# Merging two matmuls of a block product over 512 columns, and a mask fused with its row extremum, in a hand-ordered attention and MLP kernel

## The chip, the core and the metric

The kernel runs on one core of a Trainium2 chip. The core has engines with queues of their own: TensorE (PE; its weight loads are listed as PEld), VectorE (DVE), ScalarE (ACT), GpSimd (POOL) and SyncE (SP, which here issues nearly all DMAs). Matmuls write PSUM, which has eight banks of 128 partitions by 512 float32 columns; the other engines copy results out to SBUF. The metric is the device time of one execution in microseconds (us), less is better. A difference is told as a ratio of times with its interval.

## The reference

Attention over 4 sequences of 768 tokens with 8 heads of 64, each query seeing a window of fewer than 16 tokens to either side and 24 summaries of blocks of 32 keys; its output, 3072 tokens by 512, goes through an MLP.

```python
def _attn_ref(q, k, v):                       # q, k, v: (4, 8, 768, 64)
    ...
    k_sum = k.reshape(B, H, nb, block, D).max(axis=3)      # block = 32
    v_sum = v.reshape(B, H, nb, block, D).mean(axis=3)
    scores_l = scale * np.matmul(q, k.transpose(0, 1, 3, 2))
    mask_l = np.abs(pos[:, None] - pos[None, :]) < window  # window = 16
    scores_s = scale * np.einsum('bhsd,bhnd->bhsn', q, k_sum) + np.log(block)
    scores_all = np.concatenate([np.where(mask_l, scores_l, -1e9), scores_s], axis=-1)
    a = np.exp(scores_all - np.max(scores_all, axis=-1, keepdims=True))
    a = a / (np.sum(a, axis=-1, keepdims=True) + 1e-09)
    return np.matmul(a, np.concatenate([v, v_sum], axis=2))

def _moe_ref(x, w_in, w_out):                 # x: 3072 x 512, w_in: 512 x 2048
    h = x @ w_in
    sp = np.maximum(h, 0.0) + np.log1p(np.exp(-np.abs(h)))
    return (h * erf(sp)) @ w_out
```

## The kernel before

**Tiles.** The 3072 tokens are 6 chunks of 512 (`NCH`). A *quad* is one chunk by two heads, so there are 24 quads. A *period* k is one chunk by one group of 512 of the 2048 hidden columns, so there are 24 periods (`NPER`), four to a chunk. In period k the kernel computes the hidden tile of period k, the second product (`mm2`) of period k-1, and the attention of a later quad, so that PE has work of several kinds at all times.

**Float32 in two parts.** Values go through PE as a high part and a low part in a fast float32 format: w x = w_h x_h + w_h x_l + w_l x_h. So each product is three matmuls. In `mm2` (L936) and in the first product of the early periods (`mm1`, L780) they have 512 columns.

**Block products.** From period 8 (`FAST`) on, the first product is done by a scheme with seven products of 2 x 2 blocks instead of eight (`products`). For each half n (called a and b) of the group there are seven jobs P1 to P7, each over two slices c of the contraction. A job issues six matmuls of 256 columns (L821). P1, P6, P7 and P4 use bank b of their half, its left 256 columns only (`L`); P2, P5 and P3 use bank a. Bank b is `h1` for half a and `pB` for half b; `pA` and `pB` also hold the attention scores of a quad. Behind each job, small operations (`out1`, `out6`, ...) copy or add the bank's half into `hc`. The x blocks are in `xt` (the two parts of one slice lie side by side in one tile), and the sums and differences of x blocks in a place of the weights' tile (`place`, written by `tsplit`).

**Behind the products.** ScalarE makes softplus of `hc`, then erf (each behind a load of its function table, L1206); VectorE multiplies (`gsplit`: L912), casts to the high part (L257) and subtracts for the low part (L919), per half; these feed `mm2` of the next period. `hc` of a half has one buffer: the products of period k+1 can only be copied into it behind the subtraction of period k.

**Attention.** Scores of a quad are eight blocks of 64 queries for two heads, 120 columns each (96 window keys, 24 summaries), in the banks `pA` and `pB`. The first four quads get their mask on PE. From quad 4 (`MQ`) on, `softmax` adds the mask on VectorE (`add`, L589, two instructions of 480 columns), takes the maxima (`red`, L594) and scales them by -0.125 (L613); ScalarE takes the exponentials (`exps`, L604, eight instructions, each with its sum read out), VectorE normalises (L620), and from quad 12 on VectorE turns 32 x 32 blocks (L567), which are moved into place by 16 small copies on either engine.

**The order.** Nothing is issued as written. `P.add` collects every operation with a number, the engines it may run on with a planner's cost in us, and the resources that it reads and writes. The string `ORDER` then lists all numbers in the order of issue, made in advance; a `d` or `a` behind a number puts an operation that may run on two engines on VectorE or ScalarE. Each engine executes its own operations in that order, whatever becomes ready first. `FILL` maps numbers to a count of filler matmuls (L975, 256 bfloat16 columns of zeros into a spare bank) that PE issues ahead of that operation; this holds until the first `mm2` that needs the spare bank.

```python
for i, (m, l) in enumerate(((0, 0), (0, 1), (1, 0))):
    nc.tensor.matmul(shape, lhsT=w[m], rhs=y[l], start=first and c == 0 and i == 0, ...)
```

Of the kernel before, what the change touches and what calls it, by code (L numbers as in the profile page):

```python
# [26 lines left out]
T = 512  # L27
# [24 lines left out]
149 183 130 184 131 219 115 153 178 132 146 179 190 180 181 150a 177 185 151d 191 198 186 182a 133a 200 187d 134a 201 142 135 195a 188 202 145 136 203
143 205 189 192 206 152 196d 207 197 138d 137a 233 154 139 237 155d 140 234 157 175 248 238 199 211 144 156d 204a 158 208 212 159 242 160 235 220 239
213 227 243 223 241 214 209d 215 245 231 161d 224 247 162d 163 277 164 246 210 216 217 218 232 226 236 225 240 165 276 244 249 166 282 283 222 278
167a 168d 230 314 279 288 169 280 170 289 284 274 281d 285 350 171d 172a 221 286d 353 173 287 357 228d 250d 229d 252 352 305 366 351 256d 313 304 355
258 306 356 312 307 384 262a 293 174 354 308 294 251a 275 290 309 385a 253 361 295 291a 301 254 365 292 360 255 364 296 257d 297 342 320 315 259 316
343 317 264 318 310a 298 260 299 300 359 302 311a 319a 363 261 268a 263a 326 270 321 265 327 303 322 368d 269d 266 323 271 331 324a 267 272 344 358
347 332 345 380 369a 362 346 325 370 328 333 392 339 371 329a 393 334 375d 372 394 330 348d 395 335 373 387 349d 388 382 386 389 374d 390 273 451 340
455 376 381 367 449 336 377 453 337 338 450 378 417 454 341 398 391a 379 396a 452 399 418d 456 383 397 419 403 420 404 415 414 421 467 422 405 465 460
468 457 461 406 539 459 407 471 463 400 416d 464 401d 411 423 402 458 462 472a 408 409 410 425 469 426 473 424a 431 412 470 427 432 521 540 436 413  # L60
522 437 447 446 519 523 438 525 439 526 440 428 520 429d 433 448d 474 430 434d 444 475 441 435 476 442 443 524 466 479 480 477 445 535 487 485 478a
481 536 488a 482 486 490 489 541 491 483a 501 484 528 503 514 515 532 543 529 504 527 547d 531 505 548 530 506 545d 534 555 546 495 551d 533 556d 552
496 549d 497 557 550 498 553 537 492 507 508 509 516a 493 606 494a 538 610 499a 554 569 500 621 542 598 558 623 559 637 622 502 544 624 607 625 517
511d 560 626 510a 570 561 513 512 608 562d 612 599 585 627 638 685 574 601 600 575 587 518 576 740 628 577 588 563 605 571 611 602d 564 572a 589 565
590 573 566 609 805 613 578d 846 616 567d 614 618 629 615 591 592 593 619 568 620 931 579 630 586 635 631 653 594d 603 595d 597 617 596 654 580 639
581 632 647 640d 648 633 649 641 634 582 650 710 693 583d 604 692 712 584 696 713 636 711 694 714 697 642 715 643 716 655 698 695 717 656a 699 644 718
708 657 645 721 669 719 646a 702 722 687 651a 688 703 652 720 671 700 723 701 724 705 738 672 704 663 727 726 664 689d 706 742 658 673 659 743d 674
660 725 744 661 665 728 666 729 662a 814 675 667a 730 813 668 676 731 818 677 670 817 732 679 690 678 683 812 680d 739 816 682 681 707 733 815 709 735
756 758 734 684 691 745 757 736 746 750 759d 737 828 751 686 752 753 829 741 830 747 831 748 850 832 819 749a 851 772 754a 842 833 755 760 761 808 807
766 834 767 774 844 823 762 835 820 775 836 763 856 764 839 768 776 857 765a 769 840 777 864 821 858 841 825 837 773 809d 838 891 800d 945 822 810  # L70
770a 799 778 798 852 824 779 802 848 853 803 895 854 806 826 804 771 855 892 847 849 862 780 896 863a 827 845 801 893 781 843 897 867 785d 796a 791d
859 792a 874 795a 868 794a 787d 790a 860 811 866 784a 783d 788a 870 861 782a 869a 890 871a 786d 865a 894 793d 875a 789d 876 797d 948 872 877 878 873a
884 879 946 882 885d 888 880 883 929 900 881 947 930 949 932 939 936 926d 925d 886 927 928 943 887a 961 889 898 899 955d 962 956 941 901 933 950 934
938 942 963 940 902 951a 944 937 953a 952 967 964 957a 1050 969 954 968a 958 903 971 965 904 966 972 973 970d 975 974d 977 976d 979 978d 935a 905 981
906 980a 907 983 960 959 982 985 1051 984 987 986 908 989 1052 991 990d 910a 909d 995 915a 914d 924d 922a 996 916d 919a 911d 993 997 1036 998 988 1056
999 920d 913d 1000 917d 992a 923d 1054 1001 921d 912d 918d 1002 1003 1053 994 1004 1058 1005 1006 1039 1038 1034 1043 1031a 1041 1030d 1035 1055 1032
1044 1033 1007 1045 1046 1059 1047 1008 1061 1009 1048 1049 1060 1064 1149 1062 1066 1042 1065d 1068 1063 1069 1040a 1010 1037 1067a 1070 1011 1072
1134 1057 1071a 1074 1012 1073a 1155 1076 1075a 1013 1078 1077a 1080 1079 1023a 1082 1016d 1022a 1150 1081 1018a 1084 1083 1019a 1233 1086 1027a 1151
1028a 1015d 1088 1020a 1255 1029d 1021d 1092 1087d 1085 1090 1093 1026d 1094 1024d 1014d 1017d 1095 1089a 1025d 1153 1096 1097 1098 1091 1157 1099
1100 1152 1158 1101 1340 1154 1102 1137 1103 1136 1132 1142 1140 1127 1104 1143 1129a 1133 1144 1128 1131 1145 1105 1160 1106 1146 1147 1130 1148 1159  # L80
1163 1249 1161 1165 1138a 1141 1164a 1107 1162 1139a 1167 1168 1108 1135 1166a 1169 1109 1156 1171 1173 1170d 1172a 1110 1175 1174a 1177 1176a 1112d
1115a 1121d 1179 1111d 1123a 1125d 1124a 1181 1178 1250 1126a 1122d 1120d 1116a 1183 1182 1259 1118d 1185 1180 1113a 1251 1187 1184 1186d 1191 1260
1189 1192 1119d 1114d 1193 1117d 1253 1188d 1194 1195 1196 1190 1265 1197 1198 1199 1266 1252 1254 1200 1267 1201 1235 1202 1236 1231 1242 1228a 1239
# [78 lines left out]
def block_attention_mlp(ctx: ExitStack, tc: tile.TileContext, q_t, k_nat, k_win, v_tok, v_nat, v_win, w_in, w_out, out):  # L162
# [417 lines left out]
    def softmax(qd, banks=PA):  # L580
# [5 lines left out]
        def add(e):  # L586
            t = s["pr"] = prob[:, :, 0:NK]
            for a in range(2):
                e.tensor_tensor(t[:, NI * a:NI * a + NI], s["sc"][a][:, 0:NI * NK].rearrange("q (i c) -> q i c", i=NI), mk, op=ALU.add)  # L589
# [658 lines left out]
```

## Time and profile before

| | |
|---|---|
| runs (median of 3) | 613.16 us (612.96 to 619.82) |
| the profiled execution, its own time | 616.26 us |
| its span, first to last instruction | 614.5 us |
| mean granted TensorE clock | 0.997 |
| busy: PE, PEld, DVE, ACT | 99%, 83%, 77%, 75% |
| instructions: PE, DVE, ACT | 4720, 800, 911 |
| DMA | 150.22 MB, mean 244 GB/s |

Busy shares are means over stages that differ. The windows view gives, for each stretch of the span, the busy time of each engine with the number of its instructions, the granted clock, and the DMAs' share. In the timeline and in the chain of work a row begins with its start in us and its length; in brackets stands how long the engine was idle before it and what released it. The rows of a group have count, busy time and mean duration in ns.

### The profile page before, as it was taken

How to read it: one execution, taken by the hardware profiler on the slowest of the kernel's cores; microseconds unless marked ns; L12 is line 12 of the kernel's file. 1: busy time of each engine (PE TensorE's matmuls, PEld its weight loads, DVE VectorE, ACT ScalarE, POOL GpSimd, SP SyncE). 2: the span in 40 equal slices, each digit the busy share in tenths (PEclk: the TensorE clock that was granted, in tenths of full speed). 3: DMA queues.
4: the chain of work that ended last, by engine and by line, in shares of the span. 5: the costliest groups of instructions: out<-in, count | busy, mean ns of one | idle time of the engine just before them, and what ended most of it. 6: DMA issues, size and time to landing. Idle time of an engine off the chain costs nothing.

```text
span 614.5 us, 12005 instructions
## 1 busy us (share of the span) xinstructions
PE 606.9 (99%) x4720; PEld 509.6 (83%) x4720; DVE 476.0 (77%) x800; ACT 459.7 (75%) x911; POOL 4.7 (1%) x29
## 2 busy tenths in 40 slices
PE   8999999999999999999999999999999999999997
PEld 5787557888888888889889889898898898899886
DVE  3787999967989998879889979689688776545442
ACT  4879889969687978977977888977794876552360
POOL 3000000000000000000000000000000000000000
PEclk9899999999999999999999999999999999999999
DMA  8999874855755598989856876756786654575612
GB/s 305 243 394 352 330 262 143 327 181 183 255 161 207 181 373 306 351 308 296 284 219 221 311 264 219 277 216 219 271 287 223 231 177 174 213 267 174 236 69 68
DMA packets 36843, 150.22 MB, mean 244 GB/s; under 512 B 3956, under 2 KB 9396, under 8 KB 26292
## 3 DMA queue, kind: packets, MB, share of 16 engines
q1 hardware_dynamic: 36212, 148.94, 69.3%
q8 instruction: 37, 0.61, 0.4%
q10 hardware_dynamic: 576, 0.52, 0.3%
q14 instruction: 18, 0.15, 0.1%
HBM read 124.12 MB, written 23.07 MB: 240 GB/s over the span
## 4 chain that ended last, share of the span: by engine, by line
PE 93%; DMA 2%; DVE 2%; ACT 1%; issue 0%; SPq 0%; DVEq 0%; ACTq 0%
PE ops L936 39%; PE h L780 15%; PE hb L821 14%; PE ha L821 10%; PE ops L932 5%; PE px L663 4%; PE pA L544 3%; DMA vt<-v_tok 1%; DMA kw<-k_win 1%; PE pA L634 1%; PE vs L480 1%; PE pB L634 1%; ACT pr L604 0%; ACT prf L604 0%; PE h L544 0%
## 5 line engine op out<-in xcount | busy, mean ns | idle before, releaser
L936 PE MATMUL ops<-w,gh 128*128 128x512 f32 x704 | 229.5, 394 | 0.0
L936 PEld LDWEIGHTS ops<-w,gh 128*128 128x128 f32 x704 | 132.6, 188 | 28.0 <-issue 0.6
L936 PE MATMUL ops<-w,gl 128*128 128x512 f32 x352 | 137.6, 391 | 0.0
L1206 ACT ACT_TABLE_LOAD x103 | 132.1, 1283 | 1.8
L780 PE MATMUL h<-x,w 128*128 128x512 f32 x384 | 96.6, 399 | 0.0
L912 DVE TENSOR_TENSOR hc<-wt,hc 128x1024 f32<-128x1024 f32 x44 | 53.5, 1222 | 47.8 <-ACT wt L900 47.7
L780 PEld LDWEIGHTS h<-x,w 128*128 128x128 f32 x384 | 70.8, 188 | 16.8 <-issue 1.9
L936 PEld LDWEIGHTS ops<-w,gl 128*128 128x128 f32 x352 | 66.2, 188 | 12.3
L604 ACT ACTIVATE pr<-pr,stats 128x120 f32<-128x120 f32 x160 | 61.0, 382 | 8.5 <-DVE stats L613 8.2
L821 PE MATMUL hb<-w,ws 128*128 128x256 f32 x384 | 57.2, 285 | 0.4 <-ACT hc L257 0.3
L919 DVE TENSOR_TENSOR gl<-hc,gh 128x1024 fp32r<-128x1024 f32 x44 | 53.7, 1220 | 1.2 <-ACT gh L257 0.5
L257 ACT COPY hc<-hb 128x256 f32<-128x256 f32 x54 | 19.6, 368 | 43.3 <-DVE gh L257 13.8
L821 PEld LDWEIGHTS hb<-w,ws 128*128 128x128 f32 x384 | 50.5, 192 | 1.6 <-ACT hc L257 0.7
L900 ACT ACTIVATE wt<-wt 128x1024 f32<-128x1024 f32 x48 | 50.2, 1059 | 0.5
L257 ACT COPY ptr<-tb 32x256 f32<-32x256 f32 (+1 forms) x81 | 32.7, 404 | 18.3 <-DVE tb L567 17.3
L888 ACT ACTIVATE wt<-hc 128x1024 f32<-128x1024 f32 x32 | 33.4, 1058 | 12.0 <-DVE hc L257 11.8
L257 DVE CAST gh<-hc 128x1024 fp32r<-128x1024 f32 x39 | 26.9, 690 | 9.5 <-PE ops L936 8.6
L257 DVE COPY ptr<-tb 32x256 f32<-32x256 f32 (+1 forms) x111 | 31.6, 284 | 2.2
L604 ACT ACTIVATION_READ_ACCUMULATOR pr<-pr,stats 128x1 f32 x160 | 29.9, 187 | 0.0
L932 PE MATMUL ops<-a32s,gw 128*128 128x512 f32 x64 | 29.2, 596 | 0.0
L821 PE MATMUL ha<-x,ws 128*128 128x256 f32 x192 | 28.3, 284 | 0.0
L821 PE MATMUL ha<-w,ws 128*128 128x256 f32 x192 | 28.2, 283 | 0.0
(157 smaller groups left out, 916.2 us busy)
## 6 DMA issues: line engine op xcount, KB each, us to landing
w<-dr SPq DMA_DIRECT2D x36, 1024.0 KB
ws<-ds SPq DMA_DIRECT2D x30, 1024.0 KB
kw<-k_win SPq DMA_DIRECT2D x20, 480.0 KB
dr<-w SPq DMA_DIRECT2D x8, 1024.0 KB
ds<-ws SPq DMA_DIRECT2D x8, 1024.0 KB
rw<-w_in SPq DMA_DIRECT2D x8, 1023.8 KB
rw<-w_out SPq DMA_DIRECT2D x8, 1023.8 KB
vw<-v_win SPq DMA_DIRECT2D x20, 384.0 KB
```

What stands on the lines that cost most here:

```text
L257: e.copy(o, i) if e is nc.scalar else e.tensor_copy(o, i)
L604: nc.scalar.activation(s["pr"][:, j], s["pr"][:, j] if qd >= MQ else s["sc"][j // NI][:, i * NK:(i + 1) * NK], AF.Exp, scale=0.125, bias=s ...
L663: nc.tensor.matmul(shape, lhsT=s["vw"][:, j, r], rhs=y, start=True, stop=True)
L780: nc.tensor.matmul(hs[k, f][:, 0:T], lhsT=w[m], rhs=xt[ch, cc][x], start=(cc == 0 and n == 0), stop=(cc == 3 and n == 2))
L821: nc.tensor.matmul(shape, lhsT=w[m], rhs=y[l], start=first and c == 0 and i == 0, stop=c == 1 and i == 2, skip_group_check=True)
L888: nc.scalar.activation(wt[k, n], hc[k, n], AF.Softplus)
L900: act(0.96, lambda n=n: nc.scalar.activation(wt[k, n], wt[k, n], AF.Erf, scale=-1.0 if k < SOFT else 1.0), [s], [s], table=("sig",), after ...
L912: e.tensor_tensor(hc[k, n], wt.pop((k, n)), hc[k, n], op=ALU.mult)
L919: e.tensor_tensor(gs[k, n][1], hc.pop((k, n)), f32(gs[k, n][0]), op=ALU.subtract)
L932: nc.tensor.matmul(os_[ch, t], lhsT=x[0][:, i % 2, t * 128:(t + 1) * 128], rhs=w32["o", g, i // 2][:, i % 2], start=first, stop=last)
L936: nc.tensor.matmul(os_[ch, t], lhsT=x[y][:, i % 2, t * 128:(t + 1) * 128], rhs=w[m], start=first and n == 0, stop=last and n == 2)
L1206: nc.scalar.preload_act_table_set(sets[loaded])
```

## The change

1. In `products`, a job of bank b no longer issues w_h x_h and w_h x_l as two matmuls of 256 columns. One matmul of w_h over 512 columns (x_h and x_l side by side, `both_`) fills the whole bank: left half w_h x_h, right half w_h x_l. A matmul of 256 columns adds w_l x_h to the left half. So a job has four matmuls (512, 256, 512, 256). Jobs of bank a stay.
2. As the bank's right half now holds a part of the result, a new operation `rest` behind each of out1, out6, out7 and out4 adds it into `hc` on VectorE (256 columns).
3. From quad 4 on, mask, scaling by -0.125 and row extremum are one `tensor_tensor_reduce` per block of 120 columns, eight per quad, in place of two additions, one reduction and one scaling. The stored scores are then -0.125 times the masked scores, the row value is their minimum, and the exponential uses scale -1.
4. Casts (`cast`), copies of x (`xeng`) and of h (`heng`) may run on ScalarE in all periods.
5. `ORDER` and `FILL` are new. There are 88 operations more (128 `rest` more, 40 in `softmax` fewer). Among what moves: at the start, the loads of q and k for quads 2 and 3 (two heads each) go ahead of the load of the first weight, the scores of quad 2 go ahead of the exponentials of quad 1, and the normalising of quad 1 goes from ScalarE to VectorE. 12 of the casts of `gsplit` and 17 of the copies out of the banks go from VectorE to ScalarE.

```diff
-FILL = {20: 7, 48: 5, 40: 19, 61: 2, 62: 2, 94: 7}
+FILL = {20: 9, 48: 12, 60: 20, 61: 6, 62: 8, 94: 11}
 ORDER = """
...
-        def add(e):
-            t = s["pr"] = prob[:, :, 0:NK]
-            for a in range(2):
-                e.tensor_tensor(t[:, NI * a:NI * a + NI], s["sc"][a][:, 0:NI * NK].rearrange("q (i c) -> q i c", i=NI), mk, op=ALU.add)
+        def masked(e):
+            t, s["mx"] = prob[:, :, 0:NK], stat(0, par)
+            s["pr"] = t
+            for j in range(NB):
+                a, i = divmod(j, NI)
+                e.tensor_tensor_reduce(out=t[:, j], in0=s["sc"][a][:, i * NK:(i + 1) * NK], in1=mk[:, i], scale=-0.125, scalar=3e38, op0=ALU.add, op1=ALU.min, accum_out=s["mx"][:, j:j + 1])
...
         if qd >= MQ:
-            on({"DVE": 1.2}, add, banks, [pr])
-        on({"DVE": 1.06 if qd >= MQ else 1.14}, red, [pr] if qd >= MQ else banks, [f"mx{par}"])
+            on({"DVE": 2.0}, masked, banks, [pr, f"mx{par}"])
+        else:
+            on({"DVE": 1.14}, red, banks, [f"mx{par}"])
...
             o = where_[n, x][:, z]
+            if x == "b":
+                for c in range(2):
+                    w, y, both_ = what(n, c)
+                    nc.tensor.matmul(where_[n, x].rearrange("p (m f) -> p m f", m=2) if len(both_.shape) == 3 else where_[n, x].rearrange("p (m n f) -> p m n f", m=2, n=2),
+                                     lhsT=w[0], rhs=both_, start=first and c == 0, stop=c == 1, skip_group_check=True)
+                    shape = o.rearrange("p (n f) -> p n f", n=2) if len(y[0].shape) == 3 else o
+                    nc.tensor.matmul(shape, lhsT=w[1], rhs=y[0], start=False, stop=c == 1, skip_group_check=True)
+                return
...
-            pe(0.72, lambda: go(n, x, what, z, first), r(n), [pair_banks(n)["ab".index(x)]])
+            pe(0.72 if x == "a" else 0.694, lambda: go(n, x, what, z, first), r(n), [pair_banks(n)["ab".index(x)]])
...
+        def rest(n, i, z, x):
+            on({"DVE": 0.34}, lambda e: e.tensor_tensor(hc[k, n][:, i, z], bank(n, "b")[:, R], hc[k, n][:, i, z], op=ALU.add), [pair_banks(n)[1]], [x])
...
             on(light, cp, [pair_banks(n)[1]], [f"hc{n}", f"ha{n}"])
+            rest(n, 0, L, f"ha{n}")
...
-        cast = {"DVE": 0.605, "ACT": 0.95} if k < FAST else {"DVE": 0.605}
-        xeng, heng = ({"DVE": 0.6, "ACT": 0.48},) * 2 if k < early else ({"DVE": 0.6},) * 2
+        cast = {"DVE": 0.605, "ACT": 0.95}
+        xeng, heng = ({"DVE": 0.6, "ACT": 0.48},) * 2
```

More of the change, by code (lines that the diff above doesn't have):

```diff
@@ L52 @@
[L52 to L71, printed above, removed]
@@ new lines @@
+116 142 130 149 115 190 183 131 150d 184 153 132 178 191 198 179 133d 180 135 134a 185 177 192 151a 181 136 152 186 182d 143 232 138d 187d 236 146
+137d 188 189 200 154 201 139 202 140 203 197 230 246 199 144 234 195a 176 196a 204a 231 211 205 212 225 155a 206 207 208 157 213 235 156d 218 158 233
+162d 175 221 238 242 161a 214 215 159 216 222 239 223 229 160 209a 243 210 286 163 167d 237 164 224 287 169 275 274 280 168a 281 247 170 276 220 272
+240 244 228 165 171d 172d 173 344 166 248a 241 174 245 250 249a 273 345 310 349 219 251 282 254d 255a 226d 277 256 252 278 227d 257 260a 346 253 258
@@ new lines @@
+394 416d 397 395a 403 396 509 407 398 406 513 417 418 399 419 404 420 452 421d 510 408d 514 422 400 401 402 464 405 465 466 456 423 451 507 459 477
+511 424 508 460 512 478a 425 528 523 479 428 434 426a 524 518 437 436 516 427 529 429 515 519 469 533d 470 430 534 467 435 520 468d 522 438d 471 539d
+535a 472 431 540 432 433 480 473a 481 474 482 475 485 531 536 486 487 488 476 543 517 521 544d 541 483 545 525 491 537a 526 591 538 503 595 484d 530
+502 493 593 489a 597 490 492 584 542 546 505 498a 499d 623 532 547 504d 500 592 501 607 596 608 551 494 559 548 549 610 552 560d 609 553 561 554 506
@@ new lines @@
+726 651 716 652 727d 729 653a 728 730 719 675 756 717 654 667 691 758 789 718 797 790 689 668 723 795 670 693 799 720 725 847 759 731 742 721 801 810
+732 813 734 812 735 791d 811 796 743a 736 760 814 737 761 832 815 794 733a 762 738a 798 816 739 745 833 746 817 747 744 748 818 750 826 819 751 752
+820 753 763 821 800 804 838 749a 824 754a 808 822 755 802 806 839d 933 785 805 823 840 786 757 827 788 844 792 780 829 809 765d 781 767a 803 841 778a
+773a 807 845a 768d 830 880 846 825 769d 764a 881 831 782a 774d 882 842a 783 886 775d 771a 784 852 776a 766d 834 770d 851 777d 772a 853d 860 835 779a
@@ new lines @@
+993 909d 988 994 990 995 996 1048 997 1030 998 1050 999 1049 1047 1052 1000 1055 1053a 1001 1032 1033 1002 1028 1037 1025a 1035 1029 1038 1039 1134
+1003 1040 1024d 1041 1155 1026 1027 1042 1054 1043 1058 1031 1056a 1149 1061 1004 1051 1005 1034a 1057 1064 1059a 1036 1065 1060 1062a 1239 1066 1069
+1063 1261 1067a 1006 1071 1070a 1074 1068 1072a 1007 1076 1075a 1079 1073 1021a 1077 1017a 1081 1014d 1150 1013a 1078 1084 1019d 1022a 1082 1009a
+1016d 1086 1018a 1151 1083 1080 1089 1010d 1094 1087d 1020d 1095 1088 1015d 1092 1096 1352 1097 1012d 1153 1023d 1098 1011d 1008d 1099 1085 1100 1090d
@@ new lines @@
+1091 1101 1157 1093 1102 1152 1103 1158d 1154 1159 1104 1137 1136 1105 1132 1142 1140 1133 1143 1129a 1144 1130 1106 1145 1127 1160 1146 1147 1131
+1128 1148 1135 1163 1255 1161d 1156 1166 1138a 1164a 1107 1141 1162 1169 1170 1165 1167d 1171 1108 1168 1109 1174 1172a 1176 1175a 1173 1110 1179
+1177a 1181 1180a 1178 1115a 1184 1117d 1114a 1182 1111a 1116d 1186 1256 1183 1120a 1124d 1189 1112a 1187 1265 1139d 1191 1188 1257 1121a 1185 1126a
+1194 1113d 1192d 1199 1190 1200 1193 1195d 1197 1201 1119d 1196 1202 1118d 1198 1122d 1203 1125d 1123d 1259 1266 1204 1205 1206 1207 1260 1271 1258
@@ new lines @@
+1208 1274 1272a 1209 1242 1241 1210 1237 1248 1245 1238 1249 1250 1233 1211 1273 1251 1252 1234d 1253 1232 1235 1254 1236 1263 1277 1212 1275d 1368
+1269 1280 1213 1276 1278a 1246 1243a 1283 1267 1244a 1264 1284 1281a 1279 1282 1285 1268 1288 1270 1286a 1287 1290 1289a 1214 1293 1291a 1247 1292
+1295 1294a 1215 1298 1300 1296 1223a 1369 1230d 1219a 1303 1297 1217a 1301 1227d 1305 1222a 1370 1302 1218a 1299 1308 1225d 1306a 1313 1226d 1229d
+1314 1307 1220d 1311 1224d 1315 1216d 1231d 1316 1221d 1304 1372 1317 1228d 1318 1309d 1240 1319 1310 1320 1262 1382 1312 1321 1371 1322 1383d 1384
@@ new lines @@
+1484a 1461 1470 1467 1471 1458a 1462 1457a 1472 1460 1436 1473 1485 1474 1459 1475 1486 1476 1489 1487d 1576 1492 1488 1468 1465a 1490a 1495 1466a
+1491 1496 1493a 1437 1494 1497 1438 1439 1500 1498a 1499 1502 1501d 1440 1505 1503a 1507 1469 1506a 1504 1451a 1510 1454d 1448a 1508 1441a 1455d 1512
+1577 1509 1444a 1445d 1515 1446a 1513 1447a 1452d 1517 1514 1450a 1578 1511 1449a 1520 1453a 1442d 1525 1518d 1456a 1443d 1519 1526 1516 1523 1527
+1528 1521a 1529 1580 1522 1530 1531 1532 1524 1582 1533 1579 1534 1583d 1535 1584 1563 1581 1564 1569 1559 1566 1558 1570 1536 1571 1560a 1572 1573
@@ new lines @@
+1697 1664a 1681 1695a 1666 1686 1700 1693 1701 1696 1698a 1685 1702 1699 1705 1687 1703a 1704 1707 1706a 1639 1710 1708a 1709 1712 1711a 1640 1715
+1717 1713 1653a 1780 1645d 1655a 1720 1714 1654a 1718 1650d 1722 1781 1719 1649d 1725 1716 1730 1646d 1723d 1731 1652d 1724 1732 1644d 1728 1648d
+1651d 1733 1643d 1656d 1783 1734 1721 1735 1641d 1726d 1736 1647d 1727 1642d 1737 1729 1793 1738 1782 1739 1794d 1795 1784 1740 1767 1768 1741 1772
+1770 1773 1764a 1763a 1774 1766 1742 1775 1765 1796 1776 1777 1785d 1778 1789d 1786 1799 1797d 1884 1790 1802 1798 1800a 1771 1791a 1805 1787a 1792
@@ new lines @@
+2017 2057 2015 1955d 1961a 2019 2016 2051 1951a 2013 1956a 2022 1963d 2027 2020d 1957d 2021 2028 2058 2025 2029 1953d 2018 2030 2053 1959d 2031 2023d
+2024 2032 2033 2026 2063 2034 2035 2052 2064d 2036 2065 2054 2042 2038 2037 2043 2039d 2044 2055 2041 2040 2045 2059 2066 2061 2046 2047 2060 2048
+2062 2069 2056 2121 2072 2067d 2070a 2071 2075 2068 2076 2077 2073d 2074 2080 2078a 2079 2082 2081d 2085 2083a 2084 2087 2086a 2090 2088 2089 2092
+2122 2091 2095 2093 2094 2097 2123 2096 2100 2098a 2099 2105 2101a 2103 2102 2106 2107 2108 2109 2104 2110 2125 2111 2112 2113 2124 2126 2135 2114
@@ new lines @@
+2236 2234d 2235 2241 2237d 2239 2242 2238 2243 2240 2244 2261 2245 2246 2247 2262 2263 2248 2249 2260 2266 2264a 2250 2251 2265 2252 2253 2254 2255
+2256 2269 2267a 2321 2272 2270d 2271 2275 2268 2276 2277 2273d 2274 2280 2278a 2279 2282 2281a 2285 2283a 2284 2287 2286d 2290 2288 2289 2292 2322
+2291 2295 2293 2294 2297 2296 2300 2298a 2299 2305 2301a 2303 2302 2306 2307 2308 2309 2304 2310 2323 2311 2312 2313 2324 2325 2314 2315 2328 2326a
+2316 2317 2327 2318 2319 2320 2331 2329d 2332 2330 2333 2334 2335 2336 2337 2338 2339 2340 2343 2341 2344 2342 2347 2345 2348 2346 2351 2349 2352 2350
@@ L121 @@
+2353 2354
 """
@@ L610, in softmax @@
         if qd >= MQ:
-            on({"DVE": 1.2}, add, banks, [pr])
-        on({"DVE": 1.06 if qd >= MQ else 1.14}, red, [pr] if qd >= MQ else banks, [f"mx{par}"])
-        on({"DVE": 0.09}, lambda e: e.tensor_scalar(s["mx"], s["mx"], -0.125, None, op0=ALU.mult), [f"mx{par}"], [f"mx{par}"])
+            on({"DVE": 2.0}, masked, banks, [pr, f"mx{par}"])
+        else:
+            on({"DVE": 1.14}, red, banks, [f"mx{par}"])
+            on({"DVE": 0.09}, lambda e: e.tensor_scalar(s["mx"], s["mx"], -0.125, None, op0=ALU.mult), [f"mx{par}"], [f"mx{par}"])
         s["exps"] = act(3.05 if qd >= MQ else 2.77, exps, [f"mx{par}"] + ([] if qd >= MQ else list(banks)), [pr, f"sm{par}"], table=("log", "exp"))
@@ L667, in block_attention_mlp @@
     NX = 2 * NP - 1
-    pairs = {}
+    pairs, xt_both = {}, {}
     def xsplit(qd, eng):
@@ L833, in ts, with ts_both @@
             return [place(i, m)[:, c] for m in range(2)]
+        def ts_both(i, c):
+            return kept["i", i, 0][:, :, c].rearrange("p m (n j f) -> p j m n f", n=2, j=2)[:, 1]
         def x_res(p):
@@ L863, in out1 @@
             on(light, cp, [pair_banks(n)[1]], [f"hc{n}", f"ha{n}"])
+            rest(n, 0, L, f"ha{n}")
         def out6(n):
             on(light, lambda e: copy(e, hc[k, n][:, 0, R], bank(n, "b")[:, L]), [pair_banks(n)[1], f"ha{n}"], [f"hb{n}"])
+            rest(n, 0, R, f"hb{n}")
         def out5(n):
@@ L872, in out7 @@
             on({"DVE": 0.34}, lambda e: e.tensor_tensor(hc[k, n][:, 1, R], bank(n, "b")[:, L], hc[k, n][:, 1, R], op=ALU.add), [pair_banks(n)[1]], [f"hd{n}"])
+            rest(n, 1, R, f"hd{n}")
         def out3(n):
@@ L878, in out4 @@
             on(light, lambda e: copy(e, hc[k, n][:, 1, L], bank(n, "b")[:, L]), [pair_banks(n)[1], f"ha{n}"], [f"hf{n}"])
+            rest(n, 1, L, f"hf{n}")
         outs = {"P1": out1, "P6": out6, "P5": out5, "P7": out7, "P3": out3, "P4": out4}
```

101 lines of the change are left out of this document (41 added, 60 removed).

## The prediction

> **What bounds the kernel now.** I read the page's chain first, then the windows of a few long stretches, then the chain and the timeline of single periods, and last the waits.
>
> ```profile
> span 614.5 us, 12005 instructions
> ...
> PE 93%; DMA 2%; DVE 2%; ACT 1%; issue 0%; SPq 0%; DVEq 0%; ACTq 0%
> ```
>
> ```profile
> core 0: us, PE busy (x) PEld busy (x) DVE busy (x) ACT busy (x) POOL busy (x), PEclk, DMA share, GB/s
> 0.00:40.38 40.38, 37.06 (x541) 27.86 (x541) 24.86 (x47) 26.58 (x91) 4.66 (x29) 0.96 0.96 300
> 40.38:227.80 187.42, 187.42 (x1227) 141.39 (x1227) 164.44 (x244) 157.92 (x282) 0.00 (x0) 1.00 0.70 250
> 227.80:509.00 281.20, 280.42 (x2322) 249.56 (x2322) 236.40 (x442) 229.33 (x479) 0.00 (x0) 1.00 0.75 261
> 526.25:589.20 62.95, 62.95 (x398) 57.28 (x397) 30.39 (x42) 27.30 (x36) 0.00 (x0) 1.00 0.60 217
> ```
>
> TensorE carries 93% of the chain that ended last. Four stages differ. To 40.38 us the first quads are fed, and PE is short of work. To 227.8 PE never stops. From 227.8 to 509 the block products run beside attention: PE is full, VectorE is busy 236.4 of 281.2 us (84%) and ScalarE 229.3 (82%). Behind 526.25 attention is over, and VectorE is at 48% (30.39 of 62.95). So the time is PE's work, plus what PE loses at the start, plus waits that a fuller VectorE may force.
>
> **The change part by part: the merged matmuls.** The chain of a period without attention gives the price of both forms:
>
> ```profile
> 544.35 0.72 PE hb L821 x6
> ...
> 589.20 21.80 PE ops L936 x96
> ```
>
> Six matmuls of 256 columns take 0.72 us, 0.120 each; 96 of 512 columns take 21.80, 0.227 each. So 512 columns cost 13 ns less than twice 256: each matmul has a fixed part of about 13 ns. A job of bank b (P1, P6, P7, P4) has six of 256 now and two of 512 and two of 256 afterwards, 2 x 0.227 + 2 x 0.120 = 0.694 us, 0.026 less. There are 4 jobs x 2 halves x 16 periods (8 to 23) = 128: **-3.3 us**, all on the path, since PE is full there. A merged pair has no row of its own. The lower end of its gain is nothing (the fixed part stays with each 256 columns), the upper end is 3.3 by these rows, and I take 3.3.
>
> **The start.** The granted clock and the rows around its dip:
>
> ```profile
> 25.00:28.74 3.74, 3.74 (x51) 3.57 (x44) 2.86 (x7) 2.29 (x11) 0.00 (x0) 0.54 1.01 239
> ```
>
> ```profile
> 17.01 2.24 PE L975 MATMUL idle<-zeros 128*128 128x256 bf16 x19
> ...
> 23.21 0.54 PE L544 MATMUL h<-ksum,qf 64*64 64x24 f32 x23 [0.51 <-DVE ksum L474]
> 24.77 0.35 PE L544 MATMUL h<-ksum,qf 64*64 64x24 f32 x9 [1.02 <-issue]
> 25.05 1.97 PE L663 MATMUL px<-ptr,vwf 120*64 120x64 f32 x32
> ...
> 30.87 1.15 PE L663 MATMUL px<-ptr,vwf 120*64 120x64 f32 x32
> ```
>
> PE idles 0.51 and 1.02 us around the sums' scores of quad 3, and the clock then falls to 0.54 for 3.74 us: the same 32 products take 1.97 us against 1.15 later. That costs 3.74 x 0.46 = 1.7 us on the chain. The new FILL puts 14 fillers instead of 4 into this place (60: 20 instead of 40: 19, 61: 6 for 2, 62: 8 for 2), and the new order takes the normalising of quad 1 off ScalarE, where eight multiplications took 2.42 us:
>
> ```profile
> 21.56 2.42 ACT L623 ACTIVATE prf<-prf,stats 128x120 f32<-128x120 f32 x8
> 28.83 1.16 DVE L620 TENSOR_TENSOR prf<-prf,stats 128x960 f32<-128x960 f32 x1
> ```
>
> On VectorE it costs 1.16, so the exponentials of quads 2 and 3 can start earlier. The start gives between 0 (the dip returns) and 3.2 (dip 1.7 and idle 1.5 both gone). I take **-2.2**, the dip and a third of the idle time. The 24 additional fillers are 24 x 0.114 = 2.7 us of PE (2.24 for 19 in the row); the 0.51 and 1.02 us in which PE idles now hide over half of them, and the wait for the exponentials that the first 20 stand before (as the 19 do now) the rest; without that cover they would cost up to 2.7. On SP's queue the loads of q and k now go ahead of the first weight; its first use on PE is the mm1 at about 29.3, behind the dip, so I cost that at nothing. From 40.38 to 227.8 PE has no idle time to win; a lead from the start passes through unless VectorE, at 164 of 187 us there, holds it back.
>
> **VectorE in the block stage.** Each of the 128 jobs adds one addition of the bank's right half (a "rest"). The mask is rebuilt. Rows of now:
>
> ```profile
> 394.45 0.65 DVE L589 TENSOR_TENSOR pr<-pA,mask_sb 128x480 f32<-128x480 f32 x1
> 395.02 0.65 DVE L589 TENSOR_TENSOR pr<-pB,mask_sb 128x480 f32<-128x480 f32 x1
> 395.58 0.42 DVE L730 TENSOR_TENSOR traw<-px,traw 128x256 f32<-128x256 f32 x1
> 395.91 1.14 DVE L594 TENSOR_REDUCE stats<-pr 128x8 f32<-128x960 f32 x1
> 396.97 0.68 DVE L257 CAST x<-px 128x512 fp32r<-128x512 f32 x1
> 397.57 0.16 DVE L613 TENSOR_SCALAR stats<-stats 128x8 f32<-128x8 f32 x1
> 397.69 0.69 DVE L721 TENSOR_TENSOR x<-px,x 128x512 fp32r<-128x512 f32 x1
> ```
>
> By starts, a quad's mask and maximum take 0.57 + 0.56 + 1.06 + 0.12 = 2.31 us. A 256-column addition takes 0.33 between starts (395.58 to 395.91), 0.42 when the next one waits for it. From 256 to 480 columns the start-to-start time grows by 1.05 ns a column, so a block of 120 columns is at least 0.19 and eight are 1.5. For the minimum that goes out I bound from below by nothing and from above by the accumulator read on ScalarE:
>
> ```profile
> 398.07 0.19 ACT L604 ACTIVATION_READ_ACCUMULATOR pr<-pr,stats 128x1 f32 x1
> ```
>
> With a full duration, 0.42 (of 256 columns), and this 0.19 a block is 0.61, a quad 4.9. I take 2.2 for a quad, by the tiny statistics instruction of 0.12: 0.19 and some 0.09 a block. The Trainium skill's page "VectorE: DVE Perf Modes", section "Two Vector instructions with no wait between them", counts an operation that writes out its accumulator as two instructions; no row of VectorE here shows one. By that rule a quad would be 8 x (0.19 + 0.12) = 2.5, which changes the sum below by 3 us of VectorE's time.
>
> By the tags in the new order, 20 of the bank copies and 8 of the casts of these twelve periods (8 to 19) move to ScalarE:
>
> ```profile
> L257 DVE COPY hc<-hb 128x256 f32<-128x256 f32 x42 | 17.6, 419 | 5.5 <-PE hb L821 5.0
> L257 DVE CAST gh<-hc 128x1024 fp32r<-128x1024 f32 x39 | 26.9, 690 | 9.5 <-PE ops L936 8.6
> ```
>
> VectorE's load in the stretch 227.8 to 509: 236.4 + 96 rests x 0.37 (35.5) - 11 masks x 2.31 (25.4) + 11 x 2.2 (24.2) - 20 x 0.42 (8.4) - 8 x 0.69 (5.5) = 257 us of 279, 92%. It isn't the bound yet, but what used to have slack hasn't.
>
> **The added wait.** P6 of half a needs bank h1, now free only when the rest of P1a is done. In the new order this rest stands on VectorE's queue behind the subtraction of the earlier period's half b (`gsub`) in all of the periods 9 to 19. Where that subtraction stands now:
>
> ```profile
> 401.02 1.22 DVE L919 TENSOR_TENSOR gl<-hc,gh 128x1024 fp32r<-128x1024 f32 x1
> ...
> 425.15 1.22 DVE L919 TENSOR_TENSOR gl<-hc,gh 128x1024 fp32r<-128x1024 f32 x1
> ```
>
> ```profile
> 399.32 0.88 PE L821 MATMUL hb<-x,w 128*128 128x256 f32 x6
> ...
> 422.60 1.60 PE L821 MATMUL hb<-x,w 128*128 128x256 f32 x12
> ```
>
> It starts 1.70 and 2.55 us behind P1a. P6a follows P1a by 2 x 0.694 + 2 x 0.72 = 2.83 us. The rest ends 1.14 + 0.42 us behind the subtraction's start, and the hand-over takes about 0.1, so PE waits as soon as that start is later than 1.2 us behind P1a: by these two rows 0.5 and 1.4 us. The new order brings it forward somewhat (it needs 53 table loads for periods 8 to 22 instead of 62, at 1.28 us each). Following the new queues by hand with the durations above I get waits of 0.1, 0.85 and 1.0 for periods 14, 15 and 16. I take 0.6 in 11 periods, +6.6, with ends 0 and 1.4. Now, the same bank costs PE
>
> ```profile
> PEld hb L821 <- DVE hc L872: 0.8, 2, 0.5
> PEld hb L821 <- ACT hc L257: 0.7, 2, 0.5
> PEld hb L821 <- DVE hc L257: 0.7, 3, 0.3
> ```
>
> 2.2 us, which these waits replace: **+4.4 us** net, between -2.2 and +13. Behind a waiting rest VectorE's queue holds the quad's statistics and its normalising; their reader, the next period's attention product, has several us to spare. In the last four periods the rest of P1a stands ahead of that subtraction, so no wait there. From P7b to P4b PE now needs 2.11 us, and the copy-add, the rest and three hand-overs take 0.85 + 0.3 + 0.84 = 1.99 behind P7b's start: covered by 0.1; a 0.3 us block move in between would cost 0.2 a period.
>
> **The sum.** -3.3 - 2.2 + 4.4 = -1.1 us. The profiled execution took 616.26 us with a span of 614.5; the median of the runs, 613.16, is 3.1 below it, and I apply the difference to the median: 613.16 - 1.1 = **612.1 us**.
>
> **The rivals.**
> *VectorE becomes the bound (slower).* If a mask block costs over 0.53 us (the 22 us left of 279 are 2.0 more for each of 11 quads, so 4.2 a quad), VectorE can't finish in a period, and PE waits for it at every P6. For: 0.61 is the upper bound above, and 92% leaves little. Against: at 0.28 a block it is as cheap as now. At 0.61 the excess is 11 x 0.7 = 7.5 us beside the waits: 612.1 + 7.5, about 619 (615 to 623).
> *No added wait.* The order places the rests so that PE never waits on bank b: 613.16 - 3.3 - 2.2, with the old 2.2 kept or gone, 605.5 to 609, at 607.7. For: the old order, as full, lost only 2.2. Against: the subtraction's start of 1.7 and 2.55 above.
> *The dip stays.* If PE still idles over a microsecond before 25 us, the start gives nothing: 612.1 + 2.2 = 614.3.
> *The merged pair isn't cheaper*, its fixed part staying with each 256 columns: 612.1 + 3.3 = 615.4. Against: the 512-column rows. The Trainium skill's page "TensorE: Matmul & The Clock Gate", section "Back-to-back issue gap", gives columns / 2.4 + 2.5 ns, by which a job would save 5 ns and all jobs 0.6 us, near this rival; the trace's 120 and 227 ns don't agree with its 109 and 216.
>
> **How the numbers follow.** Forecast 0.42 (its own range 609.5 to 614.5), VectorE the bound 0.20, no added wait 0.23, dip stays 0.10, pair not cheaper 0.05. From 606 to 618 I leave out about a fifth of the no-wait case and half of the slower case, some 0.15. A change of 2% is 12.3 us, about what a measurement of this kernel can tell from none: under 600.9 nearly nothing reaches (0.02), over 625.4 only the slower case at its end (0.04), 0.94 within.
>
> **What would show it.** Right: 256 fewer matmuls at the block products and 24 fillers more; bank b's jobs at 0.694 in the chain; a granted clock of 1.00 from 20 to 32 us; waits of PE on bank b that name VectorE, 4 to 8 us in all, mostly P6's; VectorE at some 92% between 228 and 505. Wrong: jobs of 0.72; a dip again; mask blocks above 0.5 us; or no waits on bank b at all, when the time is near 608.

## The result, and the profile after

The changed kernel took 622.68 us (median of 4 runs, 621.72 to 624.64) beside 616.32 for the kernel before on the same chip: a ratio of 1.0104, 95% interval 1.0061 to 1.0146. It is **6.4 us slower** (3.8 to 9.0), where 1.1 us less was forecast, and it lies outside the range of 606 to 618. The profiled execution took 623.21 us. Ratios are of fast runs: they leave out one execution, of 2110.62 us, among the twelve with the new order alone.

The page of the changed kernel, its first line and its chain:

```profile
span 621.4 us, 11922 instructions
...
PE 70%; DVE 12%; ACT 11%; DMA 5%; issue 1%; SPq 0%; ACTq 0%; DVEq 0%
```

PE's share of the chain fell from 93% to 70%; VectorE, ScalarE and the DMAs now carry 28%. The windows tell in which stage (columns as before: PE, PEld, DVE, ACT, POOL busy, granted clock, DMA share, GB/s):

```profile
0.00:40.38 40.38, 39.32 (x570) 29.76 (x571) 26.13 (x49) 25.34 (x85) 4.67 (x29) 1.00 0.97 293
20.00:32.00 12.00, 12.00 (x198) 10.07 (x196) 10.55 (x22) 11.19 (x48) 0.00 (x0) 1.00 1.06 268
40.38:227.80 187.42, 187.42 (x1231) 141.92 (x1230) 158.19 (x350) 165.26 (x306) 0.00 (x0) 1.00 0.71 254
227.80:509.00 281.20, 274.03 (x2089) 232.62 (x2088) 241.53 (x620) 223.45 (x476) 0.00 (x0) 0.99 0.72 252
357.00:361.00 4.00, 3.53 (x14) 3.20 (x15) 3.49 (x8) 2.10 (x5) 0.00 (x0) 0.57 0.76 278
```

The start is what was hoped for: PE is busy 39.32 us against 37.06, and the dip of the clock is gone. The loss lies in the block stage, where PE is idle 7.2 us of 281.2 against 0.8 before, and where a new dip (0.57 over 4 us) stands at 357. VectorE is busy 86% there. The first product of period 13 starts at 352.01 and that of period 14 at 379.68, 27.67 us later; in the kernel before the same period takes 23.91 us. VectorE's timeline in that period, with PE's row of the stop:

```profile
349.95 0.41 DVE L729 TENSOR_TENSOR traw<-traw,px 128x256 f32<-128x256 f32 x1
350.28 1.22 DVE L936 TENSOR_TENSOR hc<-wt,hc 128x1024 f32<-128x1024 f32 x1
354.88 0.33 DVE L261 COPY kw<-ksum 128x96 f32<-128x96 f32 x2 [3.39 <-DMA kw<-k_win]
355.13 0.69 DVE L261 CAST gh<-hc 128x1024 fp32r<-128x1024 f32 x1
355.85 1.23 DVE L943 TENSOR_TENSOR gl<-hc,gh 128x1024 fp32r<-128x1024 f32 x1
357.00 0.42 DVE L877 TENSOR_TENSOR hc<-hb,hc 128x256 f32<-128x256 f32 x1
```

```profile
357.47 0.79 PE L826 MATMUL hb<-w,ws 128*128 128x512 f32 x1 [2.46 <-DVE hc L877]
...
407.07 0.50 PE L826 MATMUL hb<-w,ws 128*128 128x512 f32 x1 [0.76 <-DVE hc L877]
...
479.67 0.50 PE L826 MATMUL hb<-w,ws 128*128 128x512 f32 x1 [1.34 <-DVE hc L877]
```

Read it upwards. P6 of half a waits for the rest of P1 half a (357.00, line 877). That rest stands behind the subtraction (line 943), as foreseen. But ahead of the subtraction stand two **copies of key sums** into the next quad's key window, and they wait 3.39 us for the window's load. Two more copies do the same in periods 15 and 18. The chain names the load, as issue and landing:

```profile
346.56 8.30 DMA kw<-k_win
```

Before, the same load was waited for by a copy on ScalarE (one row of ScalarE's timeline of the kernel before), which held no bank of TensorE's up:

```profile
352.65 0.27 ACT L257 COPY kw<-ksum 128x96 f32<-128x96 f32 x1 [1.28 <-DMA kw<-k_win]
```

The waits between 227 and 520 us:

```profile
PEld hb L826 <- DVE hc L877: 11.7, 18, 2.7
...
DVE kw L261 <- DMA kw<-k_win: 8.0, 3, 3.4
...
PE hb L826 <- DVE hc L877: 7.0, 11, 2.5
```

The weight loads of bank b's jobs waited 11.7 us for the rests, in 18 places. PE's own rows show 7.0 us of idle time in 11 places, because a matmul's row (0.28 us at 256 columns) is longer than the step to the next start (0.12) and so hides the first part of a wait. The loads are the better measure: without a stop, these periods take 23.19 us, and period 19 22.21 (periods 14 and 19 of the run with later copies and short rests, below); here the periods 9 to 19 take 13.0 us more than that, waits and the lower clock at 357 together.

The 18 waits, one by one in the timeline of the weight loads, divide as follows. The three stops are 5.2 us. Two waits in period 10 are 1.1; ahead of them too VectorE or ScalarE waited for a DMA. Three others, at P6 of half a, are 0.8. The remaining **4.6 us, in ten periods out of eleven, are at P4 of half b**, which waits for the rest of P7b. VectorE and PE in period 17:

```profile
459.73 0.28 DVE L261 COPY ptr<-tb 32x256 f32<-32x256 f32 x1
460.04 0.43 DVE L894 TENSOR_TENSOR hc<-hb,hc 128x256 f32<-128x256 f32 x1
460.50 0.28 DVE L261 COPY ptr<-tb 32x256 f32<-32x256 f32 x1
460.81 0.42 DVE L877 TENSOR_TENSOR hc<-hb,hc 128x256 f32<-128x256 f32 x1
```

```profile
461.30 0.50 PE L826 MATMUL hb<-w 128*128 128x512 f32 x1 [0.54 <-DVE hc L877]
```

Line 894 adds the left half of P7b, line 877 at 460.81 is its rest, and between them stands a block move of the attention (460.50). Such a move stands there in all ten periods.

### The profile page after: what moved, and what is told of

It is laid out like the page before. It is cut to its first block, busy times and chain, and to the rows that moved or that the text cites. A ratio compares the mean times of both kernels' runs of the same rounds, so it can differ in the third digit from the quotient of the medians.

```text
span 621.4 us, 11922 instructions
## 1 busy us (share of the span) xinstructions
PE 609.6 (98%) x4488; PEld 497.5 (80%) x4488; DVE 491.7 (79%) x1130; ACT 468.0 (75%) x933; POOL 4.7 (1%) x29
## 4 chain that ended last, share of the span: by engine, by line
PE 70%; DVE 12%; ACT 11%; DMA 5%; issue 1%; SPq 0%; ACTq 0%; DVEq 0%
PE ops L960 28%; PE h L785 11%; PE ha L835 6%; PE hb L826 6%; PE ops L956 4%; DMA kw<-k_win 4%; ACT L1230 3%; PE px L667 3%; PE hb L829 3%; PE pA L548 2%; DVE hc L877 2%; ACT pr L607 2%; PE idle L999 2%; DVE gl L943 2%; DVE ptr L261 2%
## 5 line engine op out<-in xcount | busy, mean ns | idle before, releaser
L261 ACT COPY hc<-hb 128x256 f32<-128x256 f32 x64 | 23.6, 371 | 54.1 <-PE hb L829 44.3
L877 DVE TENSOR_TENSOR hc<-hb,hc 128x256 f32<-128x256 f32 x128 | 53.3, 418 | 10.9 <-ACT hc L261 8.8
L826 PE MATMUL hb<-w,ws 128*128 128x512 f32 x128 | 49.9, 412 | 5.6 <-DVE hc L877 5.6
L829 PE MATMUL hb<-w,ws 128*128 128x256 f32 x128 | 36.4, 284 | 0.0
L826 PEld LDWEIGHTS hb<-w,ws 128*128 128x128 f32 x128 | 24.6, 192 | 10.3 <-DVE hc L877 7.0
```

The source lines that it names most:

```text
L261: e.copy(o, i) if e is nc.scalar else e.tensor_copy(o, i)
L826: nc.tensor.matmul(where_[n, x].rearrange("p (m f) -> p m f", m=2) if len(both_.shape) == 3 else where_[n, x].rearrange("p (m n f) -> p m ...
L829: nc.tensor.matmul(shape, lhsT=w[1], rhs=y[0], start=False, stop=c == 1, skip_group_check=True)
L877: on({"DVE": 0.34}, lambda e: e.tensor_tensor(hc[k, n][:, i, z], bank(n, "b")[:, R], hc[k, n][:, i, z], op=ALU.add), [pair_banks(n)[1]], [x])
```

## The experiments

Two theories came out of this. K: a wait for a load, through copies that stand on VectorE's queue ahead of the rest. R: the load of 128 rests on VectorE. Ratios below are to the kernel before, each on one chip.

**The new order alone.** Old jobs, no rests, old mask.

```diff
- x == "b": two matmuls of 512 and two of 256, and a rest
+ x == "b": six matmuls of 256                       (new ORDER and FILL kept)
```

> Only the new order and the new fillers; bank b's jobs have six matmuls of 256 columns as before, no rest is added, and the mask is an addition, a maximum and a scaling as before. Theory K (the copies of the key sums stand on VectorE's queue ahead of the subtraction of half b and wait there for the load of the key window, which stops TensorE 2.46, 0.76 and 1.34 us in periods 13, 15 and 18, with some 1.4 us of lower clock behind the first): the stops are still there, so about +5.9 by them and -1.1 from the start, before + 3 to + 6 us, and three waits of over 0.5 us that name the window's load. Theory R (the 128 rests fill VectorE, and a bank waits for a rest behind the subtraction): no rests, no cost; before - 2.2 to 0. Theory M (the merged pair saves too little, nothing else is wrong): before - 1 to + 1.

Ratio 1.0003 (0.9973 to 1.0034), 616.6 us. K's forecast of 3 to 6 us more fails. Copies on VectorE still wait (VectorE's timeline of this run), yet no stop of PE follows them:

```profile
353.70 0.33 DVE L258 COPY kw<-ksum 128x96 f32<-128x96 f32 x2 [1.76 <-DMA kw<-k_win]
...
470.01 0.26 DVE L258 COPY kw<-ksum 128x192 f32<-128x192 f32 x1 [1.74 <-DMA kw<-k_win]
```

At 353.70 bank b is emptied by a copy on ScalarE, which does not wait; behind 470.01 a copy of VectorE's empties a bank, early enough. Periods 14 to 18 take 23.27 us, PE's work without a stop. But in period 10 the same thing happens on ScalarE, without any rest:

```profile
283.90 0.35 ACT L258 COPY kw<-ksum 128x192 f32<-128x192 f32 x1 [1.04 <-DMA kw<-k_win]
284.27 0.65 ACT L258 COPY hc<-hb 128x256 f32<-128x256 f32 x2
```

```profile
284.69 0.98 PE L823 MATMUL hb<-w,ws 128*128 128x256 f32 x6 [1.74 <-ACT hc L258]
```

A copy of key sums waits for its window, ScalarE's copy out of bank b stands behind it, and PE stops for 1.74 us. So a wait for a load reaches PE through whichever engine empties the bank; the rests put VectorE among them at every job of bank b.

**The mask alone, in both orders.**

```diff
- add; reduce max; scale by -0.125        (per quad, 2.31 us)
+ tensor_tensor_reduce per block of 120   (per quad, 1.63 us)
```

> The old order and fillers; of the change only the mask and row maximum in one instruction per block. In the changed kernel a quad's eight blocks take 1.63 us from first to last start against 2.31, 0.68 less in 20 quads. Theory K: VectorE is not the bound, so 0 to -1 us against before. Theory R: VectorE's load counts, so -1 to -3 us.

> The changed kernel's order, fillers and mask, but bank b's jobs with six matmuls of 256 columns and no rests. Both theories: no rest is there to be late, so as with the old work in this order (616.6) less 0 to 1 us. If it is over 619, the mask's form costs more than its own duration.

Ratios 1.0003 (0.9966 to 1.0040) and 1.0004 (0.9974 to 1.0034). The mask is worth nothing where no rests are, in either order: as K said for the old order, and both for the new one. In the profiled execution of the second, ScalarE's copy of period 10 waits 3.38 us for its window, and PE stops for 2.97. The reverse, the changed kernel with the old mask:

```diff
- tensor_tensor_reduce per block
+ add; reduce max; scale by -0.125        (merged jobs, rests and new ORDER kept)
```

> The changed kernel's order, fillers, merged matmuls and rests, but the mask as an addition, a maximum and a scaling as before (2.31 us a quad against 1.63). Theory K: the load is not what costs, so within 1 us of the changed kernel (622.7). Theory R: 0.68 us more on VectorE in each of 12 periods, of which PE gets half or more: 626 to 632.

It took 623.2 us, ratio 1.0124 (1.0085 to 1.0162), against 1.0104 with the new mask. R's 626 to 632 fails: 0.68 us more VectorE work in a period was not what decided. With these runs the merged jobs and their rests can be priced inside the new order, by ratios: 1.0124 less 1.0003 is 7.5 us with the old mask, 1.0104 less 1.0004 is 6.2 with the new one. They are the whole loss.

**The merged matmuls alone, in the old order.**

```diff
  out(n)                     # copy or addition of the bank's left half
+ rest(n)                    # on VectorE, directly behind it    (old ORDER else)
```

> The old order and fillers; of the change only the merged matmuls, each rest placed on VectorE's queue directly behind the copy or addition of its half, old mask. Theory K: the copies of the key sums stand as before, so only the merged pair counts: -1.3 us (128 jobs at 0.010) to 0, with PE's waits on bank b below 4 us. Theory R: 35 us more on VectorE in an order made without them: before + 3 to + 8 us, by waits on bank b that name VectorE's rest.

643.7 us, ratio 1.0446 (1.0396 to 1.0497): 27 us slower, past even R's 8. PE waited on bank b all through the stage (its waits, 227 to 520):

```profile
PEld hb L827 <- DVE hc L878: 24.5, 34, 1.3
...
PE hb L827 <- DVE hc L878: 15.8, 30, 1.1
```

So the merged jobs with their rests are what is dear, and the new order is there to carry them: it brings 27 us down to 6.

**The copies later.**

```diff
- ... kwcopy18 kwcopy18 gcast gsub ... rest1a ... norm17 ...
+ ... gcast gsub ... rest1a ... norm17 kwcopy18 kwcopy18 ...   (also quads 20, 23)
```

> The changed kernel; four copies of key sums (quads 18, 18, 20 and 23) are moved on VectorE's queue from ahead of the subtraction of half b to behind the normalising of the quad before. Theory K (what costs is the copies' wait for the key window's load, ahead of a rest): the three stops of TensorE go, 2.46 + 0.76 + 1.34 us, and the lower clock behind the first, some 1.4: 4 to 6 us less than the changed kernel's 622.7. Theory R (the rests' mean load on VectorE): the load is the same, so the changed kernel - 1 to + 1 us.

618.07 us, ratio 1.0033 (1.0007 to 1.0059), 4.6 us less than the changed kernel as K said. PE's remaining waits:

```profile
PEld hb L826 <- DVE hc L877: 6.2, 14, 0.8
```

No wait is over 0.8 us, against 2.7. Of the 6.2 us, 4.7 are at P4 of half b, in ten places, as before.

**The load earlier.** The other end of K.

```diff
- ldq(q) ldk(q)
+ ldk(q) ldq(q)              (quads 13, 14, 15, 18, 20 to 23; copies left in place)
```

> The changed kernel, but SP issues the load of the key window ahead of that of the queries for quads 13, 14, 15, 18 and 20 to 23, as nearly everywhere before; the copies of the key sums keep their place ahead of the subtraction. Theory K: 256 KB less stand ahead of the window's 480, at some 260 GB/s 1 us, so each of the three stops is up to 1 us shorter: 1 to 4 us less than the changed kernel (618.5 to 621.5). Theory R: nothing changes, 622 to 623.5.

619.63 us, ratio 1.0051 (1.0021 to 1.0081), 3 us less, within K's range. The copies in period 13 now wait 1.97 and PE 1.02 us:

```profile
354.60 0.33 DVE L261 COPY kw<-ksum 128x96 f32<-128x96 f32 x2 [1.97 <-DMA kw<-k_win]
```

```profile
357.18 0.50 PE L826 MATMUL hb<-w,ws 128*128 128x512 f32 x1 [1.02 <-DVE hc L877]
```

The waits at P4 stay, at 4.8 us.

**The rest first.** This takes away the wait that the prediction had added.

```diff
- P1a gcast gsub out1a rest1a
+ P1a out1a rest1a gcast gsub               (periods 9 to 19, later copies kept)
```

> As the run with the later copies, and in periods 9 to 19 the copy and the rest of P1 half a are placed directly behind P1 half a, ahead of the cast and the subtraction of half b. The prediction's added wait (a rest behind the subtraction) goes: 0.3 to 0.6 us in 11 periods, 3 to 6 us less than with the later copies alone. Theory R (the load, wherever the rest stands): the subtraction comes 0.4 us later, and the wait only moves to the products that read it: within 1 us of the run with the later copies.

631.83 us, ratio 1.0257 (1.0220 to 1.0295): 14 us slower than with the later copies, and both expectations miss. VectorE's waits say why:

```profile
DVE hc L877 <- ACT hc L261: 19.4, 18, 2.5
```

The rest adds to what ScalarE's copy has written, and that copy stands behind the exponentials. Put first, the rest stops VectorE's queue 18 times for 19.4 us, and everything behind it is late. Behind the subtraction, that time was covered.

**The size of the rests.** Each rest in its place, on 8 of its 256 columns (0.164 us a piece against 0.418).

```diff
- e.tensor_tensor(hc[:, i, z], bank[:, R], hc[:, i, z], op=add)
+ e.tensor_tensor(hc[:, i, z][:, 0:8], bank[:, R][:, 0:8], hc[:, i, z][:, 0:8], op=add)
```

> The run with the old order and the merged matmuls (643.7), but each rest adds 8 of its 256 columns (248 are left out), so that it stays in its place on VectorE's queue and in the chain of its bank, and costs some 0.12 us in place of 0.33. Theory R (the load of the rests is what fills VectorE): the 27.8 us over before shrink to 0.12/0.33 of them, about 10: 624 to 629. Theory H (the place is what costs: one more instruction in VectorE's order between a bank's job and its next one): most of it stays, 634 to 642.

> The run with the later copies (618.1), each rest with 8 of its 256 columns (248 are left out). Theory R: PE's remaining waits on bank b go with the load, and what is left is the new order less the merged pairs' gain: 616.6 - 1.3, about 615. Theory H: 617 to 618.

> The changed kernel in its own order, each rest with 8 of its 256 columns (248 are left out). With the later copies such rests gave 613.3. Theory K (what counts is that the first rest of a period stands behind copies that wait for the key window's load, whatever its size): the stops in periods 13, 15 and 18 stay, so 613.3 + 4 to 6 = 617 to 619. Theory R (the stops only decide because VectorE is full): 613 to 615.

In the old order: 624.44 us, ratio 1.0125 (1.0078 to 1.0173), so of 27 us some 20 went with the rests' length, as R said. In the order with the later copies: 613.33 us, 0.9943 (0.9919 to 0.9966), 5 us less than with whole rests, more than R said (616.6 - 1.3). In the changed kernel's own order: 616.48 us, 1.0007 (0.9979 to 1.0035), between the two theories; the stop of period 13 is there, but shorter:

```profile
355.56 0.50 PE L826 MATMUL hb<-w,ws 128*128 128x512 f32 x1 [1.29 <-DVE hc L877]
```

The four kernels make a table, in us against before (ratio less 1, times 616.5):

| | copies ahead of the subtraction | copies later |
|---|---|---|
| whole rests | +6.4 (the changed kernel) | +2.0 |
| rests of 8 columns | +0.4 | -3.5 |

Between the columns, the copies' place costs 4.4 (± 3.1) and 3.9 (± 2.3); between the rows, the rests' length costs 6.0 (± 3.1) and 5.5 (± 2.2). So K holds, beside a cost of the rests themselves, and the two nearly add.

That second cost is not R's load as such. Rests of 8 columns make two things smaller: VectorE's load, and the way from P7b over its rest to P4b. With them no wait at P4 is left in either order, against 4.6 and 4.7 us with whole rests. With the old mask, VectorE had more to do and the way stayed: 4.3 us at P4, and a time 0.5 us longer. This speaks for the way. That the block move in it is to blame is read from the timeline and not shown, for no run has the moves elsewhere.

**The new start alone.**

```diff
  new ORDER and FILL up to the normalising of quad 3
- new ORDER
+ old ORDER of all that is left             (old jobs, old mask)
```

> The new order and fillers up to the normalising of quad 3, and the old order behind it; old matmuls, old mask. Theory S (the fillers and the order at the start make the dip of the clock rarer, and the new order of the block stage costs 1 to 2 us): a mean clock of 0.999 or more in over half of the runs, against a quarter of before's, and the median 1 to 2.5 us under before. If the start is worth nothing: before +/- 0.7, with clocks as before's.

Ratio 0.9986 (0.9958 to 1.0014), 616.1 us. S's forecast of the clock holds, that of the time (1 to 2.5 us less) just fails. The mean granted clock was 0.999 or 1.00 in all 12 runs. Of 88 runs of the kernel before, beside the experiments, 24 had it (median 614.0 us), and 64 had 0.997 or less (617.3). So the new start makes the dip rarer, and the kernel before differs by 3.3 us between runs with and without it, with it in three of four; but at full clock the new start is 2.1 us slower than the old one, and the two nearly cancel. It does not rule the dip out: in the profiled execution of the run with the rest first, which has the new start too, the granted clock is 0.57 from 27 to 31 us, behind an idle time of PE of 1.70. And the new order has a dip of its own: with the old work 4 of 12 runs, with the new mask 6 of 12 had a clock of 0.997 or less, and in the profiled one of the latter it stands at 288 us (0.67 over 4 us), behind the stop of 2.97 us in period 10.

No kernel of these beats the one before by more than its interval, but for the one that leaves 248 of 256 columns of each rest out; the rests can't be had at that price.

## Why the prediction was wrong, step by step

**The base: 613.16.** The median of three runs was taken, 3.1 us below the profiled execution's 616.26. The 88 later runs have a median of 616.5, near the profiled one. Of the 10.6 us between 612.1 and 622.68, 3.2 are this; the other 7.5 are the change, +6.4 for -1.1.

**The merged matmuls: -3.3 forecast, about -1.3 measured.** The term "a job of bank b ... 0.694 us" was mis-sized. The chain of period 21 after:

```profile
547.19 0.23 PE hb L826
547.42 0.12 PE hb L829
547.54 0.24 PE hb L826
547.78 0.12 PE hb L829
547.90 0.71 PE ha L835 x6
```

A 512-column matmul between 256-column ones takes 0.23 to 0.24, not the 0.227 of a stream of its kind, and the job 0.71, as long as the unmerged job beside it (0.71), to the two digits of this view. The last periods are 20.90 us against 20.98 in every run with and without merging, so a job gains 0.010 us, 128 jobs 1.3 us. The prediction's rival "the merged pair isn't cheaper", at 0.05, was nearer than its forecast of 26 ns a job. The Trainium skill's page "TensorE: Matmul & The Clock Gate", section "Back-to-back issue gap", gives columns / 2.4 + 2.5 ns for a matmul by itself, from which an estimate of 5 ns a job follows; the rows show 10.

**The start: -2.2 forecast, -0.9 (-2.6 to +0.9) measured.** The dip and its price were right (fillers and order were changed together, so which of them makes it rarer is open), but one profile was read as the kernel: the dip is there in some executions and not in others. And where the clock is full anyway the new start costs 2.1 us. That fits 24 fillers without the cover that the prediction gave them (2.7), but no run has the fillers alone.

**VectorE's load.** A quad's mask takes 1.63 us, not 2.2:

```profile
347.13 0.28 DVE L595 CUSTOM_DVE_ANT_0 pr<-pA,mask_sb 128x120 f32<-128x120 f32 x1
347.33 0.08 DVE L595 DVE_READ_ACCUMULATOR2_ANT stats<- 128x1 f32 x1
347.33 0.28 DVE L595 CUSTOM_DVE_ANT_0 pr<-pA,mask_sb 128x120 f32<-128x120 f32 x1
```

A block takes 0.20 from start to start; the accumulator's row lies beside the next block's. The Trainium skill's page "VectorE: DVE Perf Modes", section "Two Vector instructions with no wait between them", counts an operation that writes out its accumulator as two instructions. The trace agrees, with two rows a block; what it does not show is the 0.12 us that the prediction put on the second one by that rule (0.31 a block). The load was 86%, not 92%, and the rival of VectorE as the bound, by a dear mask, failed (mask alone: no difference).

**The added wait: +4.4 forecast, 9.5 measured; this step failed.** The 9.5 are the 11.7 us of the weight loads less the 2.2 of the kernel before, and they lie elsewhere than forecast. The step put 0.6 us into each of 11 periods, 6.6 in all, as a wait of P6a for a rest behind the subtraction. Where no late load stood ahead, that wait came to 0.8 us, in three places. Two other things took its place.

First, what stands ahead of the subtraction. The step followed VectorE's queue from the subtraction to the rest, and took the subtraction's start from the old order. In the new order, copies that wait for a DMA stand in front of it in periods 13, 15 and 18, and the waits there are 5.2 us. Moving only these copies takes 4.6 us off (4.4 by ratios), and loading their data about a microsecond sooner 3. The prediction asked what is queued behind the waiting rest; it should have asked what the rest is queued behind, back to the last thing that waits for another engine or a load.

Second, the way from P7b to P4b. The step called it "covered by 0.1", priced a block move in between at 0.2 us a period, and put nothing into the sum. The move is there in ten periods, and the wait is 0.46 on average, 4.6 us in all; with rests of 8 columns it is gone.

That 11.7 less the three stops, 6.5, lies so near the forecast 6.6 is luck: 4.6 of it are the waits at P4.

**What stays open.** The parts (-1.3 pair, -0.9 start, +1.1 for the rest of the new order, which is the new order alone less the new start alone, 0 mask, +4.4 copies, +5.5 length of the rests) sum to +8.8, 2.4 over the measured 6.4; the intervals are wider than that. In the old order, rests of 8 columns are still 7 us slower than before; the weight loads wait 12.0 us for rests there (227 to 530 us), but why was not taken apart.

## What to carry to other kernels

Merging two matmuls saves the first engine its fixed part (10 ns here) and gives the second one a whole instruction (0.33 us here): count both, and take the price of a mixed stream from mixed rows. When an instruction gets a reader that TensorE waits for, follow its queue backwards to the nearest DMA wait, on whichever engine it runs, for one copy that could idle for microseconds unnoticed turns into a stop. Where a chain between two jobs is covered by only 0.1 us, put what else stands between its links on the queue into the sum. And a dip of the clock in one profile is a property of that execution until a second one shows it.

## What the runs showed of the hardware

A stop of PE of 2.46 us was followed by a granted clock of 0.57 over the next 4 us (the window at 357.00 above), and the stop of 2.97 us with the new order and mask by 0.67 (288 to 292). The stop of 1.74 us with the new order alone left it at 1.00 (284.7 to 288.7), as did the one of 1.29 us in the changed kernel's order with rests of 8 columns:

```profile
355.50:359.50 4.00, 3.94 (x27) 3.66 (x28) 3.55 (x11) 3.13 (x8) 0.00 (x0) 1.00 0.85 312
```

The landing of one and the same transfer moves. The 480 KB of period 13 landed 8.30 us after the issue in the changed kernel; with the old work in the same order, SP's issue is

```profile
346.64 0.41 SPq L502 DMA_DIRECT2D kw<-k_win  x1
```

and the copy that waits for it starts at 353.70 (shown above), so it landed some 7.0 us later. Why it took 1.3 us more wasn't tried.
